# Attention ahead of two expert layers: two pairs of score banks that change roles from tile to tile, and chunks of the product with V that end with a tile

## The chip, the cores and the metric

The kernel runs on one core of a Trainium2 chip. The metric is the device time of one execution in microseconds (us); the kernel before has a median of 1350.61 us over three runs (1348.88 to 1350.84). A core has five engines that work side by side, each through its own queue in program order, and wait for each other by semaphores: TensorE (PE; its weight loads are listed apart as PEld), VectorE (DVE), ScalarE (ACT), GpSimd (POOL) and SyncE (SP, which here only starts transfers). Matmul results land in PSUM, which has eight banks; a bank holds 512 fp32 numbers in each of 128 partitions.

## The reference

The program computes attention and then two mixtures of experts. The change touches attention alone:

```
q_pool = q.reshape(B, H, S // 2, 2, D).mean(axis=3)      # B, H, S, D = 4, 8, 1152, 64
scores = scale * np.matmul(q_pool, k.transpose(0, 1, 3, 2))
scores = scores - np.max(scores, axis=-1, keepdims=True)
attn = np.exp(scores)
attn = attn / (np.sum(attn, axis=-1, keepdims=True) + 1e-09)
out = np.matmul(attn, v)
```

## The kernel before, in words

Two heads of one batch element make a pair; there are 16 pairs. A pair has 2 x 576 pooled queries, cut into nine tiles (t = 0 to 8) of 128, so there are 144 steps g = 9 * pair + t. A row of scores has 1152 entries, three parts of 384; each part fills most of a PSUM bank.

The list `SEQ` (line 17) says what each step issues, and in which order. Step g works on two tiles at once: it makes the scores, maxima and exponentials of tile g + 2, and takes tile g, whose exponentials lie in SBUF, through the rest.

- `qk(g+2, n)` (L158): matmuls of a score part. A part is the sum of two matmuls with 384 columns (for t = 4, whose rows belong to two heads, of four). `q0` makes the first two parts in the tile `Sa` (two banks, one buffer), `q1` the third in `Sb` (one bank, two buffers).
- `smax`, `bias` (L174, L177): DVE takes the maxima of `Sa` and of `Sb`, and of both the negative maximum `bs`.
- `exp` (L180): ACT takes the exponential of `Sa` (768 wide) and then of `Sb` (384 wide), each with a sum over the row; such an exponential is two instructions, ACTIVATE and ACTIVATION_READ_ACCUMULATOR, and the second one signals that the bank is free.
- `tp` (L212): PE transposes tile g in three groups of three into three `T` banks (L216). `evH` (L226): ACT rounds each group into `PH` (L227). `evL` (L228): DVE writes the remainder into `PL` (L229), which frees the `T` bank.
- `takeav` (L275): PE takes some of the pending matmuls with V (L239). The rows of a pair form four chunks of two or two and a half tiles; a chunk is 18 matmuls into the bank `O`, which has one buffer, and the last one is followed by a copy `O` to `xo` on ACT (L242). The table `AVN` says how many are taken at each t; they are taken in two halves, at `av` (between the second and the third cast on ACT) and at `aw` (behind the exponentials).
- `prep`, `inv`: transposes and copies for the pairs to come, which take a `T` bank too, and the transposed sums of the rows.

A step's `q0` may write `Sa` only when the step before has taken the exponential of its `Sa`. The eight banks are two for `Sa`, two for `Sb`, three for `T` and one for `O`. In the second half of the stage `dec` puts decoding of the expert weights into steps.

Of the kernel before, what the change touches and what calls it, by code (L numbers as in the profile page):

```python
# [10 lines left out]
F32=mybir.dt.float32; F32R=mybir.dt.float32r; I32=mybir.dt.int32; U32=mybir.dt.uint32; I64=mybir.dt.int64; BF16=mybir.dt.bfloat16  # L11
AF=mybir.ActivationFunctionType; ALU=mybir.AluOpType; AX=mybir.AxisListType
PSUM=bass.MemoryType.PSUM; DRAM=bass.MemoryType.DRAM

SEQ='q1 q0 m1 sum dec t0 c0 m0 pool scl t1 c1 bias l0 t2 av c2 l1 e0 e1 l2 aw prep inv st'.split()
AVN=(9,3,10,7,11,7,10,7,8)
PREP={0:((1,'T0'),),2:((1,'T1'),),3:((1,'T2'),),5:((1,'q2'),),7:((2,'q0'),),8:((2,'q1'),)}
POOL={0:((0,'vH1'),(0,'vL1')),1:((1,'H0'),(1,'L0')),3:((1,'H1'),(1,'L1')),4:((1,'H2'),(1,'L2')),5:((2,'qadd'),),6:((2,'qH'),(2,'qL')),8:((1,'vH0'),(1,'vL0'))}  # L20
SPQ={4:((1,'D0'),),7:((1,'D1'),)}
SCALE=(7,8,11,12)
CFG=dict(S2=1,S1=2,T=3,O=1)
def attention(tc, q, k, v, xS, rS, ident, pairs=None, extra=(), start=lambda: None):
    nc=tc.nc
    B,H,S,D=q.shape
    NP=H//2; SQ=S//2; KT=S//128
    if pairs is None: pairs=[(b,hp) for b in range(B) for hp in range(NP)]
    ctx=contextlib.ExitStack()
    with ctx:  # L30
# [4 lines left out]
        kv=ctx.enter_context(tc.tile_pool(name="a_kv",bufs=1))  # L35
        pr=ctx.enter_context(tc.tile_pool(name="a_pr",bufs=1))
        ld=ctx.enter_context(tc.tile_pool(name="a_ld",bufs=1))
        psS=ctx.enter_context(tc.tile_pool(name="a_psS",bufs=CFG['S2'],space=PSUM))
        psU=ctx.enter_context(tc.tile_pool(name="a_psU",bufs=CFG['S1'],space=PSUM))
        psT=ctx.enter_context(tc.tile_pool(name="a_psT",bufs=CFG["T"],space=PSUM))  # L40
        psO=ctx.enter_context(tc.tile_pool(name="a_psO",bufs=CFG["O"],space=PSUM))

# [6 lines left out]
        def load(i,what="qkv",eng=None):  # L49
            if i>=len(pairs): return  # L50
            b,hp=pairs[i]; h0=2*hp
            d=D_.setdefault(i,dict(ks={},vs={},kst={}))
            for w in what:
                if w=='q':
                    t=d['qn']=ld.tile([128,KT,2,D],F32,name="qn")
                    (eng or nc.sync).dma_start(out=t,in_=q[b,h0:h0+2].rearrange("h (s r) d -> (h s) (r d)",r=2).rearrange("(t p) x -> p t x",p=128))
                else:
                    t=d[w+'n']=ld.tile([128,2,KT,D],F32,name=w+"n")
                    (eng or nc.sync).dma_start(out=t,in_={'k':k,'v':v}[w][b,h0:h0+2].rearrange("h (p t) d -> p h t d",p=128))
# [89 lines left out]
        st={}  # L149
# [3 lines left out]
        def new(g):  # L153
            nm=sm.tile([128,2],F32,name="nm",bufs=3); bs=sm.tile([128,1],F32,name="bs",bufs=3)
            P=pp.tile([128,S],F32,name="P")
            st[g]=dict(nm=nm,bs=bs,su=sus[:,(g//9)%2,g%9],P=P,S={})

        def qk(g,n):  # L158
            i,t=divmod(g,9); d=D_[i]
            if g not in st: new(g)  # L160
            A=QA[i%2]; Bq=QB[i%2]
            if t==4: L=[(512,0),(640,1)]
            else: L=[(128*t,0)] if t<4 else [(128*t+128,1)]
            ops=[(w[:,c:c+128],h) for c,h in L for w in (A,Bq)]
            if n==0:
                o=psS.tile([128,2,512],F32,name="Sa"); st[g]['S'][0]=o[:,:,0:384]
                outs=[(o[:,j,0:384],j) for j in range(2)]
            else:
                o=psU.tile([128,384],F32,name="Sb"); st[g]['S'][1]=o
                outs=[(o,2)]  # L170
            for o,j in outs:
                for x,(w,h) in enumerate(ops):
                    nc.tensor.matmul(o,w,d['kst'][h][:,j*384:(j+1)*384],start=(x==0),stop=(x==len(ops)-1))  # L173
        def smax(g,n):  # L174
            s=st[g]
            nc.vector.tensor_reduce(out=s['nm'][:,n:n+1],in_=s['S'][n],axis=AX.XY if n==0 else AX.X,op=ALU.max,negate=True)  # L176
        def bias(g):  # L177
            nm=st[g]['nm']
            nc.vector.tensor_reduce(out=st[g]['bs'],in_=nm,axis=AX.X,op=ALU.min)  # L179
        def exp(g,n):  # L180
            s=st[g]; P=s['P']
            o=P[:,0:768].rearrange("p (c x) -> p c x",x=384) if n==0 else P[:,768:1152]
            nc.scalar.activation(out=o,in_=s['S'][n],func=AF.Exp,bias=s['bs'],scale=1.0,accum_out=s['su'][:,n:n+1])  # L183

        inv={}; rB={}
        TS=((0,5),(5,9))
# [4 lines left out]
        def invT(i,h):  # L191
            a,b=TS[h]; bb,hp=pairs[i]; n=b-a
            T=psT.tile([128,384],F32,name="T",tag="T")
            nc.tensor.transpose(T[0:n,0:128],inv.pop((i,h))[:,1,0:n],ident)
            o=sm.tile([5,128],F32,name="ro",bufs=1)
            nc.scalar.copy(out=o[0:n],in_=T[0:n,0:128])
            flat=rS[bb][hp:hp+1].rearrange("o h s -> (o h s)")
            nc.sync.dma_start(out=flat[128*a:128*b].rearrange("(t p) -> t p",p=128),in_=o[0:n])
        def invB(i,h):
            bb,hp=pairs[i]  # L200
            flat=rS[bb][hp:hp+1].rearrange("o h s -> (o h s)")
            r=rB[i,h]=sm.tile([128,576],F32,name="rB",bufs=2)
            nc.sync.dma_start(out=r,in_=flat[576*h:576*h+576].partition_broadcast(128))
# [8 lines left out]
        def tp(g,j):  # L212
            T=psT.tile([128,384],F32,name="T",tag="T"); P=st[g]['P']
            for n in range(3):
                kt=3*j+n
                nc.tensor.transpose(T[:,n*128:(n+1)*128],P[:,kt*128:(kt+1)*128],ident)  # L216
            st[g][j]=T
# [8 lines left out]
        def evH(g,j):  # L226
            for H,L,src in parts(g,j): nc.scalar.copy(out=H,in_=src)  # L227
# [29 lines left out]
        ops={}  # L257
        def do(i,*names):

            if i>=N: return  # L260
            if i not in ops: ops[i]=pool_ops(i,i==0)|prep_ops(i)
            for n in names:
                o=ops[i].pop(n,None)
                if o: o()
# [1 line left out]
        load(1)  # L266
        avq=[]; extra=list(extra); NX=len(extra); at={}
        for g in (0,1):
            for j in range(2): qk(g,j)
            if g==0: do(0,'k10','k11','k12','vH0','vL0','vH1','vL1'); do(1,'qadd','qH','qL')  # L270
            for j in range(2): smax(g,j)
            bias(g)
            for j in range(2): exp(g,j)
        DONE={1:[0],4:[1],6:[2],8:[3]}
        def takeav(n):  # L275
            while avq and n>0:
                avq[0].pop(0)(); n-=1
                if not avq[0]: avq.pop(0)
        stores=[]; sums={}
        for g in range(NG+4):  # L280
            i,t=divmod(g,9)
            if g<NG:
                if t==2 and i>0: load(i+1,'v')
                if t==2: load(i+2,'q')
                if t==5: load(i+2,'k')
            f2=g+2<NG; f0=g<NG
            if not f0:
                while avq: takeav(99)
            for op in SEQ:
                a=op[:-1]; n=op[-1]  # L290
                if op=='scl':
                    if g in at: x,y=at.pop(g); x(); stores.append((g,y))
                elif op=='st':
                    while stores and (stores[0][0]<g or not f0): stores.pop(0)[1]()
                elif op=='inv':
                    if f0 and t in (3,7): invT(i,t//4)
                    if t==5 and f0: invB(i,0)
                    if t==0 and i>0: invB(i-1,1)
                    for di,x in SPQ.get(t,()): f0 and do(i+di,x)
                    if g in (0,2): do(1,'q0' if g==0 else 'q1')  # L300
                elif not f0: pass
                elif a=='q': f2 and qk(g+2,int(n))
                elif a=='m': f2 and smax(g+2,int(n))
                elif a=='e': f2 and exp(g+2,int(n))
                elif op=='bias': f2 and bias(g+2)
                elif a=='t': tp(g,int(n))
                elif a=='c': evH(g,int(n))
                elif op in ('av','aw'): takeav((AVN[t]+(op=='av'))//2)
                elif a=='l': evL(g,int(n))
                elif op=='sum':  # L310
                    if t in (3,7): ssum(i,t//4)
                elif op in ('pool','prep'):
                    for di,n in (POOL if op=='pool' else PREP).get(t,()): do(i+di,n)
                elif op=='dec':
                    want=NX*max(0,g-70)//max(1,NG-74); take(extra,want-(NX-len(extra)))
                else: raise Exception(op)
            if f0:
                for c in DONE.get(t,[]): avq.append(av_ops(i,c))
# [702 lines left out]
```

## Time and profile before

| what | before |
|---|---|
| median of three runs | 1350.61 us |
| the profiled execution's own time | 1348.71 us |
| its span from the first to the last instruction | 1346.6 us |
| around the span | 2.1 us |
| PE busy / DVE busy / ACT busy | 1229.3 / 1095.5 / 892.2 us (91 / 81 / 66%) |
| granted TensorE clock, mean | 0.988 |

Attention takes about the first 570 us of the span. A busy share counts the time in which an instruction of the engine was under way. Matmuls overlap each other in it, and a weight load that waits for a semaphore may do so while the matmuls ahead of it still count as busy. So a stretch may show PE busy all the time and be set by something else; how long a step takes is read from the times at which the same instruction starts in one step and the next.

### The profile page before, as it was taken

The numbers are of one execution on the slowest core, as the hardware profiler recorded it, in microseconds if no ns is written. First come the engines' busy times: TensorE is split into PE (matmuls) and PEld (weight loads), VectorE is DVE, ScalarE is ACT, GpSimd is POOL, SyncE is SP. The second block draws the span as 40 slices with busy tenths as digits, with TensorE's granted clock in tenths as the row PEclk, the third lists the DMA queues.
The fourth block names the chain that finished last, engine by engine and source line by source line (L and its number), as shares of the span: only waits on it lengthen the run. The fifth ranks groups of instructions, "written<-read, shape, count | busy, mean of one in ns | idle before, by whom it ended". The sixth has DMA issues, their size and how long they took to land. (4 is left out here: it accounts for less than half of the span.)

```text
span 1346.6 us, 22379 instructions
## 1 busy us (share of the span) xinstructions
PE 1229.3 (91%) x7341; PEld 1084.1 (81%) x7341; DVE 1095.5 (81%) x1970; ACT 892.2 (66%) x2059; POOL 635.6 (47%) x567
## 2 busy tenths in 40 slices
PE   5999999999999999977768989899999999999997
PEld 4888888888888888865657879797989887788885
DVE  5788888888888888789997697848485889998894
ACT  6888888888888888744445645454556657576772
POOL 3444444444555555256667443424342435455852
PEclk9999999999999999989898999999999999999999
DMA  5554555556555575244331311010101323258710
GB/s 165 141 143 127 128 154 138 139 142 168 152 151 137 132 187 140 58 139 117 109 102 48 109 41 36 25 40 16 40 17 47 138 72 138 94 191 328 278 36 22
DMA packets 119624, 154.34 MB, mean 115 GB/s; under 512 B 12135, under 2 KB 93943, under 8 KB 115152
## 3 DMA queue, kind: packets, MB, share of 16 engines
q1 hardware_dynamic: 115232, 140.93, 36.7%
q0 software_dynamic: 3696, 11.34, 2.4%
q8 instruction: 60, 0.98, 0.3%
q10 hardware_dynamic: 576, 0.59, 0.1%
q14 instruction: 60, 0.49, 0.1%
HBM read 155.48 MB, written 20.28 MB: 131 GB/s over the span
## 5 line engine op out<-in xcount | busy, mean ns | idle before, releaser
L430 PE MATMUL h<-xH,W 128*128 128x384 f32 (+1 forms) x896 | 229.0, 327 | 51.5 <-ACT yt L439 37.5
L227 ACT CAST PH<-T 128x384 fp32r<-128x384 f32 (+1 forms) x480 | 185.7, 460 | 84.7 <-PE T L216 84.6
L229 DVE TENSOR_TENSOR PL<-T,PH 128x384 fp32r<-128x384 f32 (+1 forms) x480 | 217.4, 508 | 6.4 <-ACT PH L227 6.3
L430 PEld LDWEIGHTS h<-xH,W 128*128 128x128 f32 x896 | 161.8, 195 | 72.3 <-ACT yt L439 48.3
L453 POOL TENSOR_TENSOR gL<-et,gH 128x384 fp32r<-128x384 f32 (+1 forms) x112 | 120.1, 1072 | 197.7 <-ACT gH L452 170.1
L818 DVE TENSOR_TENSOR W<-sg,W 128x2048 fp32r<-128x2048 f32 (+1 forms) x84 | 193.9, 2341 | 14.1 <-POOL W L816 7.2
L435 ACT ACTIVATE em<-h 128x384 f32<-128x384 f32 (+1 forms) x112 | 49.8, 445 | 224.4 <-DVE et L444 149.5
L239 PE MATMUL O<-PH,vs 128*128 128x256 f32 (+1 forms) x576 | 166.3, 311 | 17.9 <-ACT xo L242 17.9
L176 DVE TENSOR_REDUCE nm<-Sa 128x1 f32<-128x768 f32 x144 | 136.8, 950 | 40.6 <-PE Sa L173 35.1
L216 PE MATMUL T<-ident,P 128*128 128x128 f32 x1296 | 164.8, 272 | 0.0
L239 PE MATMUL O<-PL,vs 128*128 128x256 f32 (+1 forms) x576 | 161.9, 303 | 0.0
L216 PEld LDWEIGHTS T<-ident,P 128*128 128x128 f32 x1296 | 150.1, 140 | 5.2
L430 PE MATMUL h<-xL,W 128*128 128x384 f32 (+1 forms) x448 | 144.0, 321 | 0.7 <-DVE xL L385 0.7
L444 DVE SCALAR_TENSOR_TENSOR et<-em,et 128x384 f32<-128x384 f32 (+1 forms) x112 | 69.5, 621 | 84.4 <-ACT em L441 82.8
L183 ACT ACTIVATE P<-Sa,bs 128x768 f32<-128x768 f32 x144 | 133.6, 928 | 4.1 <-DVE bs L179 3.9
L173 PE MATMUL Sa<-kst,qa 128*128 128x384 f32 x320 | 114.5, 358 | 16.7 <-ACT P L183 14.8
L239 PEld LDWEIGHTS O<-PH,vs 128*128 128x128 f32 x576 | 108.6, 189 | 25.6 <-ACT xo L242 23.9
L817 ACT CAST W<-sg 128x2048 fp32r<-128x2048 f32 (+1 forms) x63 | 114.2, 1835 | 15.0 <-DMA sg<-moe_w 15.0
L461 PE MATMUL y<-W,gH 128*128 128x512 f32 x288 | 115.7, 402 | 0.0
L176 DVE TENSOR_REDUCE nm<-Sb 128x1 f32<-128x384 f32 x144 | 79.8, 554 | 42.6 <-PE Sb L173 41.7
L462 PE MATMUL y<-W,gH 128*128 128x512 f32 x288 | 113.8, 395 | 0.0
L239 PEld LDWEIGHTS O<-PL,vs 128*128 128x128 f32 x576 | 108.8, 189 | 0.0
(298 smaller groups left out, 2940.9 us busy)
## 6 DMA issues: line engine op xcount, KB each, us to landing
sg<-moe_w SPq DMA_DIRECT2D x80, 1024.0 KB
qn<-q SPq DMA_DIRECT2D x16, 576.0 KB
kn<-k SPq DMA_DIRECT2D x16, 576.0 KB
rB<-rS SPq DMA_DIRECT2D x32, 288.0 KB
vn<-v SPq DMA_DIRECT2D x15, 576.0 KB
dx<-moe_w_in SPq DMA_DIRECT2D x16, 512.0 KB
dx<-moe_w_out SPq DMA_DIRECT2D x16, 512.0 KB
qb<-qa SPq DMA_DIRECT2D x64, 96.0 KB
```

Of the source, the lines that this page charges most:

```text
L173: nc.tensor.matmul(o,w,d['kst'][h][:,j*384:(j+1)*384],start=(x==0),stop=(x==len(ops)-1))
L176: nc.vector.tensor_reduce(out=s['nm'][:,n:n+1],in_=s['S'][n],axis=AX.XY if n==0 else AX.X,op=ALU.max,negate=True)
L183: nc.scalar.activation(out=o,in_=s['S'][n],func=AF.Exp,bias=s['bs'],scale=1.0,accum_out=s['su'][:,n:n+1])
L216: nc.tensor.transpose(T[:,n*128:(n+1)*128],P[:,kt*128:(kt+1)*128],ident)
L227: for H,L,src in parts(g,j): nc.scalar.copy(out=H,in_=src)
L229: for H,L,src in reversed(list(parts(g,j))): nc.vector.tensor_tensor(out=L,in0=src,in1=H.bitcast(F32),op=ALU.subtract)
L239: nc.tensor.matmul(O[0][:,:n],vs[:,kt].rearrange("p a d -> p (a d)"),R[:,kt,:n],start=first,stop=last)
L430: nc.tensor.matmul(h[:,:N],a,b[:,k,:N],start=(n==0),stop=(n==11)); n+=1
L453: nc.gpsimd.tensor_tensor(out=gL[:,:N],in0=t_,in1=gH[:,:N].bitcast(F32),op=ALU.subtract)
L461: nc.tensor.matmul(y,gH[:,sl],wH,start=(f==0),stop=False)
L817: else: nc.scalar.copy(out=H[:,q],in_=s[:,q])
L818: (nc.gpsimd if (w,j,h) in self.pool_L else nc.vector).tensor_tensor(out=L[:,q],in0=s[:,q],in1=H[:,q].bitcast(F32),op=ALU.subtract)
```

## The change

It has three parts.

1. The tiles `Sa` and `Sb` are replaced by two pairs of banks, `S0` and `S1`. Tile g has its first two parts in the pair `S(g mod 2)` and its third in the first bank of the other pair. The parts are computed in the order 0, 1, 2 (`q0 q1 q2` in `SEQ`); the maximum of the first two is taken before that of the third; and the exponential of the third part (384 wide, "short") now stands ahead of that of the first two (768 wide, "long").
2. `AVN` is rewritten so that each chunk's last matmul is the last one that a step takes.
3. The transposes for the middle third of a pair's queries (`q1` in `PREP`) move from t = 8 to t = 0, where `T0` already stands.

```diff
-SEQ='q1 q0 m1 sum dec t0 c0 m0 pool scl t1 c1 bias l0 t2 av c2 l1 e0 e1 l2 aw prep inv st'.split()
-AVN=(9,3,10,7,11,7,10,7,8)
+SEQ='q0 q1 q2 m1 sum dec t0 c0 m0 pool scl t1 c1 bias l0 t2 av c2 l1 e0 e1 l2 aw prep inv st'.split()
+AVN=(6,3,9,7,11,8,10,8,10)
...
-        psS=ctx.enter_context(tc.tile_pool(name="a_psS",bufs=CFG['S2'],space=PSUM))
-        psU=ctx.enter_context(tc.tile_pool(name="a_psU",bufs=CFG['S1'],space=PSUM))
+        psS=ctx.enter_context(tc.tile_pool(name="a_psS",bufs=1,space=PSUM))
...
+        SB=[psS.tile([128,2,512],F32,name=f"S{n}") for n in range(2)]
...
-            for o,j in outs:
-                for x,(w,h) in enumerate(ops):
-                    nc.tensor.matmul(o,w,d['kst'][h][:,j*384:(j+1)*384],start=(x==0),stop=(x==len(ops)-1))
+            o=SB[g%2][:,n,0:384] if n<2 else SB[1-g%2][:,0,0:384]
+            for x,(w,h) in enumerate(ops):
+                nc.tensor.matmul(o,w,d['kst'][h][:,n*384:(n+1)*384],start=(x==0),stop=(x==len(ops)-1))
+        def score(g,n): return SB[1-g%2][:,0,0:384] if n==0 else SB[g%2][:,:,0:384]
...
-            o=P[:,0:768].rearrange("p (c x) -> p c x",x=384) if n==0 else P[:,768:1152]
-            nc.scalar.activation(out=o,in_=s['S'][n],func=AF.Exp,bias=s['bs'],scale=1.0,accum_out=s['su'][:,n:n+1])
+            o=P[:,768:1152] if n==0 else P[:,0:768].rearrange("p (c x) -> p c x",x=384)
+            nc.scalar.activation(out=o,in_=score(g,n),func=AF.Exp,bias=s['bs'],scale=1.0,accum_out=s['su'][:,n:n+1])
```

PE in the step t = 7 of the first pair, before; `O_1070` is the chunk that is under way and `O_1177` the next one.

```order
L173 MATMUL Sb_1142<-kst_1032,qa0_135 128x384
L173 MATMUL Sb_1142<-kst_1032,qb0_137 128x384
L173 MATMUL Sa_1145<-kst_1032,qa0_135 128x384
L173 MATMUL Sa_1145<-kst_1032,qb0_137 128x384
L173 MATMUL Sa_1145<-kst_1032,qa0_135 128x384
L173 MATMUL Sa_1145<-kst_1032,qb0_137 128x384
L216 MATMUL T_1154<-ident_75,P_1042 128x128 x3
L216 MATMUL T_1163<-ident_75,P_1042 128x128 x3
L216 MATMUL T_1170<-ident_75,P_1042 128x128 x3
L239 MATMUL O_1070<-PL_879,vs_715 128x320
L239 MATMUL O_1177<-PH_992,vs_772 128x320
```

The same step now; `S0` and `S1` are the two pairs, and `O_1138` is the next chunk.

```order
L168 MATMUL S0_141<-kst_999,qa0_132 128x384
L168 MATMUL S0_141<-kst_999,qb0_134 128x384
L168 MATMUL S0_141<-kst_999,qa0_132 128x384
L168 MATMUL S0_141<-kst_999,qb0_134 128x384
L168 MATMUL S1_142<-kst_999,qa0_132 128x384
L168 MATMUL S1_142<-kst_999,qb0_134 128x384
L211 MATMUL T_1118<-ident_75,P_1009 128x128 x3
L211 MATMUL T_1127<-ident_75,P_1009 128x128 x3
L211 MATMUL T_1134<-ident_75,P_1009 128x128 x3
L234 MATMUL O_1138<-PH_959,vs_745 128x320
```

The four matmuls of the pair come first and the two of the third part last; the chunk before has ended in the step before, so the step's first product opens a new one. The first `S0` matmul waits for the short exponential of the step before, and the first `S1` matmul for the long one, which has read that pair.

ACT in a step of the first pair in which a chunk ends, before.

```order
L227 CAST PH_768<-T_764 128x3x128
L227 CAST PH_768<-T_775 128x3x128
L242 COPY xo_790<-O_668 128x320
L227 CAST PH_768<-T_782 128x3x128
L183 ACTIVATE P_754,sus_141<-Sa_758,bs_753 128x768
L183 ACTIVATE P_754,sus_141<-Sb_755,bs_753 128x384
```

ACT in a step of the first pair in which a chunk ends, now.

```order
L222 CAST PH_850<-T_846 128x3x128
L222 CAST PH_850<-T_855 128x3x128
L222 CAST PH_850<-T_862 128x3x128
L178 ACTIVATE P_832,sus_138<-S0_141,bs_831 128x384
L178 ACTIVATE P_832,sus_138<-S1_142,bs_831 128x768
L237 COPY xo_880<-O_759 128x256
```

The copy of `O` has moved from between the casts to behind the exponentials, and the short exponential from behind the long one to before it.

## Rows read from the trace of the kernel before

**Rows 1.** Waits of PE, 30 to 570 us: total us, times, longest.
```profile
PE O L239 <- ACT xo L242: 17.3, 31, 0.7
PE Sa L173 <- ACT P L183: 10.3, 19, 1.6
```

**Rows 2.** Nine steps of one pair, by windows: length, busy us by engine, clock, DMA.
```profile
213.42:216.93 3.51, 3.51 (x26) 3.30 (x25) 3.06 (x6) 2.98 (x8) 0.76 (x2) 1.00 0.99 243
216.93:220.45 3.52, 3.52 (x27) 3.42 (x26) 3.02 (x7) 2.79 (x8) 1.34 (x1) 1.00 0.65 171
220.45:224.77 4.32, 3.76 (x27) 3.47 (x26) 3.19 (x9) 3.59 (x10) 2.56 (x3) 1.00 0.11 30
224.77:228.32 3.55, 3.55 (x28) 3.47 (x27) 3.07 (x7) 3.02 (x9) 3.13 (x4) 1.00 0.47 96
228.32:232.68 4.36, 3.80 (x28) 3.46 (x27) 3.15 (x7) 3.53 (x10) 0.00 (x0) 1.00 0.94 210
232.68:236.88 4.20, 3.69 (x25) 3.34 (x24) 3.03 (x7) 2.77 (x8) 2.40 (x3) 1.00 0.83 248
236.88:240.44 3.56, 3.56 (x30) 3.49 (x29) 3.02 (x7) 3.03 (x9) 0.00 (x0) 1.00 0.53 153
240.44:243.96 3.52, 3.52 (x28) 3.15 (x26) 3.20 (x9) 3.31 (x10) 2.23 (x3) 1.00 0.00 0
243.96:247.66 3.70, 3.57 (x28) 3.21 (x27) 3.23 (x10) 3.30 (x13) 2.90 (x3) 1.00 0.50 113
```

**Rows 3.** Timeline of PE, 215 to 220 us: start, length, engine, line, operation.
```profile
215.68 0.42 PE L173 MATMUL Sb<-kst,qa 128*128 128x384 f32 x1
...
216.13 0.44 PE L173 MATMUL Sa<-kst,qa 128*128 128x384 f32 x1
...
219.38 0.34 PE L173 MATMUL Sb<-kst,qa 128*128 128x384 f32 x1
...
219.74 0.35 PE L173 MATMUL Sa<-kst,qa 128*128 128x384 f32 x1
```

**Rows 4.** Timeline of ACT, 213 to 217 us.
```profile
213.95 1.25 ACT L227 CAST PH<-T 128x384 fp32r<-128x384 f32 x3 [0.56 <-PE T L216]
215.06 0.93 ACT L183 ACTIVATE P<-Sa,bs 128x768 f32<-128x768 f32 x1
215.86 0.22 ACT L183 ACTIVATION_READ_ACCUMULATOR P<-Sa,bs 128x1 f32 x1
215.95 0.60 ACT L183 ACTIVATE P<-Sb,bs 128x384 f32<-128x384 f32 x1
216.41 0.23 ACT L183 ACTIVATION_READ_ACCUMULATOR P<-Sb,bs 128x1 f32 x1
```

**Rows 5.** Timeline of PE, 222 to 236 us.
```profile
222.29 0.41 PE L239 MATMUL O<-PH,vs 128*128 128x320 f32 x1 [0.56 <-ACT xo L242]
...
235.39 0.44 PE L173 MATMUL Sa<-kst,qa 128*128 128x384 f32 x1 [0.51 <-ACT P L183]
```

**Rows 6.** Timeline of ACT, 230 to 246 us.
```profile
230.12 0.42 ACT L242 COPY xo<-O 128x320 f32<-128x320 f32 x1 [0.42 <-issue]
...
230.82 0.92 ACT L183 ACTIVATE P<-Sa,bs 128x768 f32<-128x768 f32 x1
...
234.32 0.93 ACT L183 ACTIVATE P<-Sa,bs 128x768 f32<-128x768 f32 x1
...
245.75 0.97 ACT L183 ACTIVATE P<-Sa,bs 128x768 f32<-128x768 f32 x1
```

**Rows 7.** Timeline of DVE, 217 to 220 us.
```profile
217.13 0.96 DVE L176 TENSOR_REDUCE nm<-Sa 128x1 f32<-128x768 f32 x1 [0.25 <-PE Sa L173]
218.12 0.16 DVE L179 TENSOR_REDUCE bs<-nm 128x1 f32<-128x2 f32 x1
218.19 1.48 DVE L229 TENSOR_TENSOR PL<-T,PH 128x384 fp32r<-128x384 f32 x3
219.94 0.56 DVE L176 TENSOR_REDUCE nm<-Sb 128x1 f32<-128x384 f32 x1 [0.27 <-PE Sb L173]
```

More of the change, by code (lines that the diff above doesn't have):

```diff
@@ L13 @@
 PSUM=bass.MemoryType.PSUM; DRAM=bass.MemoryType.DRAM
-SEQ='q1 q0 m1 sum dec t0 c0 m0 pool scl t1 c1 bias l0 t2 av c2 l1 e0 e1 l2 aw prep inv st'.split()
-AVN=(9,3,10,7,11,7,10,7,8)
-PREP={0:((1,'T0'),),2:((1,'T1'),),3:((1,'T2'),),5:((1,'q2'),),7:((2,'q0'),),8:((2,'q1'),)}
+SEQ='q0 q1 q2 m1 sum dec t0 c0 m0 pool scl t1 c1 bias l0 t2 av c2 l1 e0 e1 l2 aw prep inv st'.split()
+AVN=(6,3,9,7,11,8,10,8,10)
+PREP={0:((1,'q1'),(1,'T0')),2:((1,'T1'),),3:((1,'T2'),),5:((1,'q2'),),7:((2,'q0'),)}
 POOL={0:((0,'vH1'),(0,'vL1')),1:((1,'H0'),(1,'L0')),3:((1,'H1'),(1,'L1')),4:((1,'H2'),(1,'L2')),5:((2,'qadd'),),6:((2,'qH'),(2,'qL')),8:((1,'vH0'),(1,'vL0'))}
@@ L22 @@
 SCALE=(7,8,11,12)
-CFG=dict(S2=1,S1=2,T=3,O=1)
+CFG=dict(T=3,O=1)
 def attention(tc, q, k, v, xS, rS, ident, pairs=None, extra=(), start=lambda: None):
@@ L164, in qk @@
             ops=[(w[:,c:c+128],h) for c,h in L for w in (A,Bq)]
[L165 to L170, printed above, removed]
-            for o,j in outs:
-                for x,(w,h) in enumerate(ops):
-                    nc.tensor.matmul(o,w,d['kst'][h][:,j*384:(j+1)*384],start=(x==0),stop=(x==len(ops)-1))
+            o=SB[g%2][:,n,0:384] if n<2 else SB[1-g%2][:,0,0:384]
+            for x,(w,h) in enumerate(ops):
+                nc.tensor.matmul(o,w,d['kst'][h][:,n*384:(n+1)*384],start=(x==0),stop=(x==len(ops)-1))
+        def score(g,n): return SB[1-g%2][:,0,0:384] if n==0 else SB[g%2][:,:,0:384]
         def smax(g,n):
-            s=st[g]
-            nc.vector.tensor_reduce(out=s['nm'][:,n:n+1],in_=s['S'][n],axis=AX.XY if n==0 else AX.X,op=ALU.max,negate=True)
+            nc.vector.tensor_reduce(out=st[g]['nm'][:,n:n+1],in_=score(g,n),axis=AX.X if n==0 else AX.XY,op=ALU.max,negate=True)
         def bias(g):
@@ L268, in attention @@
         for g in (0,1):
-            for j in range(2): qk(g,j)
+            for j in range(3): qk(g,j)
             if g==0: do(0,'k10','k11','k12','vH0','vL0','vH1','vL1'); do(1,'qadd','qH','qL')
-            for j in range(2): smax(g,j)
+            for j in (1,0): smax(g,j)
             bias(g)
@@ L299, in attention @@
                     for di,x in SPQ.get(t,()): f0 and do(i+di,x)
-                    if g in (0,2): do(1,'q0' if g==0 else 'q1')
+                    if g==0: do(1,'q0')
                 elif not f0: pass
```

## The prediction

> **What bounds the kernel now.** I read the waits first. Within attention PE names two: 17.3 us before the first product with V of a new chunk, until ACT has copied the bank `O`, and 10.3 us before the scores, until ACT has taken an exponential [rows 1]. That looks like an engine near its limit with 28 us to win. The windows say something else. I cut one pair at the start of each step's first transpose (L216), call that moment T, and get the nine steps from t = 5 round to t = 4, in all 34.24 us [rows 2]. The reader should see that four of them last 3.51, 3.52, 3.52 and 3.56 us although their work on PE differs, and that in them PE counts as busy from end to end. Equal lengths with unequal work mean that a loop through several engines sets the step, and the timelines give its parts:
>
> - From T = 213.42 the casts begin at 213.95 and follow each other; the exponential of `Sa` begins at 215.06, which is T + 1.64 [rows 2, 4]. I call this moment E.
> - Its accumulator read ends at 215.86 + 0.22 = 216.08, E + 1.02 [rows 4]. Only then is `Sa` free.
> - The first matmul into `Sa` starts at 216.13, 0.05 later, though `Sb` was begun at 215.68 [rows 3].
> - The next T is 216.93, so four score matmuls that start from a wait take 0.80 [rows 2, 3]. Where nothing waited, from 219.74 to 220.45, they took 0.71 [rows 2, 3].
>
> The sum, 1.64 + 1.02 + 0.05 + 0.80 = 3.51, is the step. The same sum fits the odd steps. For t = 1 the next scores are those of the tile over two heads: 235.39 to 236.88 is 1.49 for eight matmuls [rows 2, 5], so each further one costs (1.49 - 0.80)/4 = 0.17, and 1.64 + 1.02 + 0.05 + 1.49 = 4.20, as measured. For t = 4 there are six casts, E is at 245.75 - 243.96 = 1.79 [rows 2, 6], and the sum is 3.66 against 3.70. For t = 0 the copy to `xo` at 230.12 stands between the casts [rows 6], E comes at 230.82 - 228.32 = 2.50, and the sum is 4.37 against 4.36. Only t = 7 (4.32) is longer than this loop: there the new chunk waits 0.56 at 222.29 [rows 5] on PE itself. So attention is bound by the loop PE, ACT, PE through the score banks, and not by PE's work.
>
> **What the change removes.** Chunks that end with a step take the copy to `xo` out from between the casts, and no product waits for it: the copy now has the rest of the step. The steps t = 0 and t = 7 then fall to the length of an ordinary step. The same 72 products per pair are issued, and PE has room for them: the step with most of them has ten of 320 columns and no other transposes, now as before, and PE came to its end at 219.38, T + 2.45 [rows 2, 3].
>
> **What it adds.** Exponential order and bank roles lengthen the loop. Both exponentials are done when the second accumulator read ends, 216.41 + 0.23 = 216.64, E + 1.58 [rows 4]; the order of the two doesn't change that sum. Before, the second one freed a bank with a spare, and nobody waited. Now the second one is the long one, and it frees the bank into which the very next step's third part goes. The first one is short: from its start to the end of its read it takes 216.41 + 0.23 - 215.95 = 0.69 [rows 4], so it frees the bank for `q0` at E + 0.69.
>
> So the next step goes: `q0` can start at E + 0.74 (that is T + 2.38), or when PE comes free, at most T + 2.45. Four matmuls end 0.80 or 0.71 later, in either case by about E + 1.54. `q2` must wait until E + 1.58 + 0.05 = E + 1.63, and its two matmuls, which again start from a wait, take 0.80 - 2 x 0.17 = 0.46. An ordinary step becomes 1.64 + 1.63 + 0.46 = 3.73 instead of 3.51. Put the other way: the freeing moment comes 0.56 later, and only two matmuls instead of four (0.34) are left behind it.
>
> For t = 1 the first wait decides, since eight matmuls stand before the third part: 1.64 + 0.74 + 1.49 + 4 x 0.17 = 4.56. For t = 4 I add the same 0.22 to the measured 3.70, which gives 3.92.
>
> **What lies beside other work.** DVE's part stays hidden. Before, the long maximum starts at T + 0.20 and the bias ends at 218.12 + 0.16, T + 1.35, so 0.29 before E [rows 2, 7]. Now the long maximum needs only the first four matmuls. These end two matmuls and a short wait before T, so it starts about T - 0.25; with 0.96 for it, 0.56 and 0.03 for the short one and 0.16 for the bias [rows 7] it ends at about T + 1.46, still 0.18 before E. The lower bound of its cost is nothing (E is set by the casts, so an earlier bias gains nothing either). The upper bound is the long maximum starting at T + 0.20 all the same: T + 1.91, so 0.27 in each step. I take nothing, being nearer to the four-matmul start that the instruction order gives it.
>
> In t = 0 two groups of three transposes now follow the products; each takes a `T` bank and so waits for a subtraction on DVE. In the sample step those begin at T + 1.26 and three take 1.48 [rows 2, 7], so the second bank comes free at about T + 2.3, and even with 0.4 for the last group the scores start by T + 2.7 and `q2` by T + 3.4, against T + 3.27 from the loop: the step ends at T + 3.75 instead of 3.73 (two unwaited matmuls take 0.35). I cost it at nothing; if the second group had to wait for all three subtractions, it would be some 0.4 us per pair, 6 us in all. Nothing is gained there, as the loop is longer than PE's work. The transfers that follow the moved transposes fill query buffers a whole pair ahead of their use and wait for nobody. On ACT the two copies and the one of `T0` follow the exponentials, where ACT otherwise waits (0.56 us at 213.95, [rows 4]).
>
> **The sum.** Seven ordinary steps at 3.73, plus 4.56 and 3.92, are 34.59 us a pair against 34.24, so 0.35 more: t = 0 and t = 7 give back 0.63 and 0.59, and the seven others take 0.17 to 0.36 each. Over 16 pairs that is 5.6. Corrections at the ends: the first pair has no chunk to end at t = 0, so it saves nothing there (0.63 + 0.21 = 0.8 more); the last pair's t = 8 has no scores left to compute (0.2 less); and four products and one copy's wait go from the tail of the stage (4 x 0.15 + 0.56 = 1.2 less). Net 5.0. The profiled execution took 1348.71 us, so the sum is 1353.7 us for it. The median shown is 1.9 above that execution; the same change from 1350.61 gives 1355.6 us, which I forecast. Its own range, 0.03 us a step either way over 142 steps, is 1351 to 1360.
>
> **Rivals.**
>
> - *PE is the bound after all.* Then the wait for `xo` is gained whole and the loop stays hidden: 1350.6 - 17.3 = 1333.3 us. For it speaks that PE counts as busy all through ordinary steps; against it that these steps are equal to 0.05 us and equal to the loop's sum. Chance 0.08. The Trainium skill's page "Perfetto Trace Analysis", section "Identifying the Most-Contended Engine", says to take the engine with the highest occupancy as the bottleneck, with a caution about TensorE, and to close the gaps on it; by that rule this rival would be the forecast, and the trace does not bear it out here.
> - *The second wait costs no restart.* If the weights for `q2` are loaded during the short wait, its two matmuls take 0.09 less (0.80 against 0.71). In eight steps of a pair that is 0.72, over 16 pairs 11.5: 1344 us, faster than before. Against it: each first matmul that followed a wait for the bank was long (0.44 against 0.35, [rows 3, 5]). Chance 0.12.
> - *The maxima arrive late*, as bounded above: 0.27 x 9 x 16 = 39, so 1394 us. It decides once the long maximum waits for the third part. Chance 0.04.
> - *The two transpose groups in t = 0 hold PE*: 1362 us. Chance 0.04.
> - *The more frequent waits lower the clock.* Against it: the granted clock is 1.00 (its upper level, 2.4 GHz) in all nine windows, with waits of 0.56 and 0.51 us in them [rows 2, 5]. At the lower level, 1.2 GHz, PE's 2.45 + 6 x 0.17 = 3.5 us of an ordinary step would double, an estimate of 3.3 us more a step and of some 470 us in all, if it lasted: 1820 us. Chance 0.01. The Trainium skill's page "TensorE: Matmul & The Clock Gate", section "A second HAM failure mode: psum-queue depth-cycling", describes a kernel whose PE paused briefly between groups of matmuls as it went through its banks, and kept losing clock; the trace of before shows none of that here.
>
> The change does what it says: the instruction order shows every copy to `xo` behind the exponentials. The remaining 0.03 is for gains and losses that cancel.
>
> **How the numbers follow.** The forecast has 0.68. A measurement of this kernel can tell about 0.2%, 2.7 us, from no change, so slower begins at 1353.3. Of the forecast's 0.68 I put 0.08 below that line; the other 0.60 and the three slower rivals' 0.09 make 0.69. Within 0.2%: 0.08 + 0.03 = 0.11. Faster: 0.08 + 0.12 = 0.20. The range goes from 1343, which takes in the rival without a restart, to 1361; outside stay PE as the bound, the late maxima and the held transposes, 0.17 with the clock.
>
> **What would show it.** In the profile after, no wait of a product for `xo`; the windows from T to T of t = 0 and t = 7 near 3.73, of t = 1 near 4.56, of t = 2, 3, 5, 6 and 8 near 3.73; the first matmul of the third part starting 0.05 after the long exponential's accumulator read, with a length of about 0.44; and the exponentials beginning at T + 1.64 everywhere. Ordinary steps of 3.6 or less, or E later than T + 1.7, would make the forecast wrong.

## The result and the profile after

The changed kernel takes 1364.87 us, median of four runs (1363.26 to 1366.16), beside 1350.38 us for the kernel before, measured next to it (four runs). The ratio is 1.0109, with a 95% interval of 1.0091 to 1.0126: slower, by 14.5 us, where 5.0 were forecast. The span of the profiled execution went from 1346.6 to 1362.0 us. The direction and the mechanism in the steady steps came out as predicted; the cost of the decoding was left out of the sum, and so was the clock at the start.

The nine steps of one pair after the change, t = 5 round to t = 4, cut from T to T as in [rows 2] (length, busy us of PE, PEld, DVE, ACT and POOL with counts, granted clock, DMA share, GB/s):

```profile
218.73:222.46 3.73, 3.73 (x27) 3.46 (x26) 2.95 (x7) 3.08 (x8) 0.83 (x2) 1.00 0.96 267
222.46:226.21 3.75, 3.75 (x27) 3.42 (x26) 3.00 (x7) 3.02 (x8) 1.26 (x1) 1.00 0.45 125
226.21:229.94 3.73, 3.73 (x29) 3.45 (x28) 3.05 (x9) 3.17 (x9) 2.51 (x3) 1.00 0.05 19
229.94:233.67 3.73, 3.73 (x27) 3.41 (x26) 3.09 (x7) 3.02 (x8) 3.20 (x4) 1.00 0.45 91
233.67:237.41 3.74, 3.74 (x29) 3.31 (x28) 2.83 (x7) 3.22 (x10) 0.00 (x0) 1.00 0.71 155
237.41:241.99 4.58, 3.69 (x25) 3.45 (x24) 3.27 (x7) 2.99 (x8) 1.52 (x2) 1.00 0.60 139
241.99:245.72 3.73, 3.73 (x28) 3.34 (x27) 2.82 (x7) 3.20 (x9) 0.88 (x1) 1.00 0.97 298
245.72:249.45 3.73, 3.63 (x27) 3.16 (x26) 3.05 (x9) 3.32 (x10) 2.27 (x4) 1.00 0.18 45
249.45:253.37 3.92, 3.75 (x27) 3.29 (x26) 3.34 (x10) 3.14 (x11) 2.87 (x3) 1.00 0.57 122
```

All seven ordinary steps last 3.73 to 3.75 us, t = 1 4.58 and t = 4 3.92. The pair takes 34.64, where 34.59 was predicted. PE again counts as busy from end to end in nearly every step, and nearly every step is 0.2 us longer: it still is not the bound.

The first of these steps on ACT and PE, T = 218.73 (start, length, engine, line, operation), answers to [rows 3, 4]:

```profile
219.26 1.24 ACT L222 CAST PH<-T 128x384 fp32r<-128x384 f32 x3 [0.77 <-PE T L211]
220.38 0.61 ACT L178 ACTIVATE P<-S,bs 128x384 f32<-128x384 f32 x1
220.85 0.22 ACT L178 ACTIVATION_READ_ACCUMULATOR P<-S,bs 128x1 f32 x1
220.94 0.92 ACT L178 ACTIVATE P<-S,bs 128x768 f32<-128x768 f32 x1
221.73 0.23 ACT L178 ACTIVATION_READ_ACCUMULATOR P<-S,bs 128x1 f32 x1
```

```profile
221.14 0.43 PE L168 MATMUL S<-kst,qa 128*128 128x384 f32 x1
...
222.01 0.44 PE L168 MATMUL S<-kst,qa 128*128 128x384 f32 x1
222.29 0.34 PE L168 MATMUL S<-kst,qb 128*128 128x384 f32 x1
222.46 1.15 PE L211 MATMUL T<-ident,P 128*128 128x128 f32 x9
```

E is at T + 1.65. The long read ends at 221.73 + 0.23 = 221.96, E + 1.58; the third part starts 0.05 later with a long first matmul (0.44), and 0.45 after that the next T follows: 1.65 + 1.58 + 0.05 + 0.45 = 3.73. Each length is within 0.01 of the predicted one. DVE in the same step, as in [rows 7]:

```profile
218.38 1.42 DVE L171 TENSOR_REDUCE nm<-S 128x1 f32<-128x768 f32 x2 [0.55 <-PE S L168]
219.84 0.16 DVE L174 TENSOR_REDUCE bs<-nm 128x1 f32<-128x2 f32 x1
```

Both maxima run without a break from T - 0.35 on, and the bias ends at 220.00, T + 1.27, which leaves 0.38 us up to E.

The waits of PE in attention, 30 to 590 us (total us, times, longest), answer to [rows 1]:

```profile
PE S L168 <- ACT P L178: 23.2, 29, 1.7
...
PE O L234 <- ACT xo L237: 0.6, 1, 0.6
```

The wait for `xo` is gone, 17.3 us to 0.6. That gain was real; the longer loop swallows it.

Where the 15.4 us of span went, by the times of T in both traces: up to T of the third tile 2.4 (30.82 to 33.21 us); from there the pairs that decoding leaves alone, up to T of t = 5 in the last pair, 5.3 (353.41 to 358.72 in all); pairs 8 to 12, where decoding lengthens steps, 8.4 (174.53 to 182.90); from T of t = 5 in the last pair to the end -0.7.

Of the 8.4, the steady pair's 0.39 (34.64 against 34.25) explains five times that, 2.0. The rest, 6.4 us, is new. Put the other way: these five pairs exceed five steady ones by 3.3 us before and by 9.7 now. One such step shows why. It is t = 4 of pair 11, T = 429.10; the next T is at 434.01, so it lasts 4.91 instead of 3.92. First DVE, then ACT:

```profile
428.89 0.96 DVE L171 TENSOR_REDUCE nm<-S 128x1 f32<-128x768 f32 x1 [0.60 <-PE S L168]
429.77 1.43 DVE L345 SCALAR_TENSOR_TENSOR dx<-dx 128x512 f32<-128x512 int32 x1
431.12 0.54 DVE L171 TENSOR_REDUCE nm<-S 128x1 f32<-128x384 f32 x1
431.70 0.15 DVE L174 TENSOR_REDUCE bs<-nm 128x1 f32<-128x2 f32 x1
```

```profile
429.84 1.22 ACT L222 CAST PH<-T 128x192 fp32r<-128x192 f32 x5
431.95 0.58 ACT L178 ACTIVATE P<-S,bs 128x384 f32<-128x384 f32 x1 [0.89 <-DVE bs L174]
```

`SEQ` has `dec` between `m1` and `m0`. A decoding instruction of 1.43 us stands between the long and the short maximum, the bias ends at 431.85, and the exponentials start at T + 2.85 with 0.89 us of waiting on ACT. This one takes more than the 0.38 us that an ordinary step has to spare. Before, [rows 7] shows DVE idle for 0.27 and 0.25 ahead of each maximum, and the short one came first: there was room for most of it.

The start of attention, windows as above. After the change:

```profile
20.00:22.00 2.00, 0.59 (x2) 0.59 (x3) 0.61 (x2) 1.32 (x3) 1.83 (x3) 0.70 0.54 200
22.00:24.00 2.00, 2.00 (x9) 1.91 (x8) 0.91 (x2) 0.24 (x2) 0.62 (x1) 0.50 0.00 0
24.00:26.00 2.00, 2.00 (x10) 1.66 (x9) 1.70 (x5) 1.30 (x3) 0.00 (x0) 0.50 0.00 0
26.00:28.00 2.00, 2.00 (x12) 1.85 (x11) 0.64 (x2) 2.00 (x8) 0.00 (x0) 0.59 0.00 0
```

The same stretch before:

```profile
20.00:22.00 2.00, 0.01 (x1) 0.01 (x1) 1.28 (x4) 1.05 (x3) 1.83 (x3) 1.00 0.51 192
22.00:24.00 2.00, 1.93 (x13) 1.66 (x13) 0.98 (x2) 1.18 (x4) 0.52 (x1) 1.00 0.00 0
```

The granted clock fell to 0.50, which is 1.2 GHz, from 20.80 to 27.63 us; in this trace of the kernel before, it stayed at 1.00.

### The profile page after: what moved, and what is told of

The parts are those of the page before. It is cut to its first block, busy times and chain, and to the rows that moved or that the text cites. A ratio compares the mean times of both kernels' runs of the same rounds, so it can differ in the third digit from the quotient of the medians.

```text
span 1362.0 us, 22402 instructions
## 1 busy us (share of the span) xinstructions
PE 1247.3 (92%) x7341; PEld 1084.2 (80%) x7341; DVE 1087.7 (80%) x1970; ACT 891.1 (65%) x2059; POOL 633.5 (47%) x567
## 5 line engine op out<-in xcount | busy, mean ns | idle before, releaser
L171 DVE TENSOR_REDUCE nm<-S 128x1 f32<-128x768 f32 (+1 forms) x288 | 208.0, 750 | 109.8 <-PE S L168 109.8
L222 ACT CAST PH<-T 128x384 fp32r<-128x384 f32 (+1 forms) x480 | 182.8, 460 | 102.8 <-PE T L211 102.3
L178 ACT ACTIVATE P<-S,bs 128x384 f32<-128x384 f32 (+1 forms) x288 | 214.6, 764 | 8.8 <-DVE bs L174 8.6
L168 PE MATMUL S<-kst,qa 128*128 128x384 f32 x480 | 185.7, 387 | 27.6 <-ACT P L178 26.4
L813 DVE TENSOR_TENSOR W<-sg,W 128x2048 fp32r<-128x2048 f32 (+1 forms) x84 | 190.3, 2298 | 17.6 <-ACT W L812 9.7
L168 PE MATMUL S<-kst,qb 128*128 128x384 f32 x480 | 162.8, 339 | 0.0
L234 PE MATMUL O<-PL,vs 128*128 128x256 f32 (+1 forms) x576 | 158.7, 299 | 0.0
L168 PEld LDWEIGHTS S<-kst,qa 128*128 128x128 f32 x480 | 90.8, 189 | 62.6 <-ACT P L178 56.4
```

Source lines behind the costliest of these rows:

```text
L168: nc.tensor.matmul(o,w,d['kst'][h][:,n*384:(n+1)*384],start=(x==0),stop=(x==len(ops)-1))
L171: nc.vector.tensor_reduce(out=st[g]['nm'][:,n:n+1],in_=score(g,n),axis=AX.X if n==0 else AX.XY,op=ALU.max,negate=True)
L178: nc.scalar.activation(out=o,in_=score(g,n),func=AF.Exp,bias=s['bs'],scale=1.0,accum_out=s['su'][:,n:n+1])
L234: nc.tensor.matmul(O[0][:,:n],vs[:,kt].rearrange("p a d -> p (a d)"),R[:,kt,:n],start=first,stop=last)
L813: (nc.gpsimd if (w,j,h) in self.pool_L else nc.vector).tensor_tensor(out=L[:,q],in0=s[:,q],in1=H[:,q].bitcast(F32),op=ALU.subtract)
```

## The experiments

Ratios are against the kernel before, measured next to each kernel, with 95% intervals.

**Decoding taken out from between the maxima** (the changed kernel):

```diff
-... m1 sum dec t0 c0 m0 ... e0 e1 l2 aw ...
+... m1 sum t0 c0 m0 ... e0 e1 l2 dec aw ...
```

> The changed kernel with one edit: the decoding of the expert weights (dec) stands behind the last subtraction of a step instead of between the long and the short maximum. Theory (decode between the maxima makes the bias and with it the exponentials late): in the pairs 8 to 12 the steps fall back to 3.73, 4.57 and 3.92 us but for a few, the 9.7 us that these pairs lie above 5 x 34.64 shrink to under 3, and the kernel takes about 1358 us. Rival (the decoding costs the same wherever it stands, through VectorE's time or a shared port): 1365 us, within 1.5. In the first 30 us the stretch at half clock stays, as nothing changes there.

Measured: 1356.32 us (1354.93 to 1356.52, five runs), 1.0042 [1.0028, 1.0056]. Pairs 8 to 12 now exceed five steady pairs by 1.9 us instead of 9.7, and ACT's waits for the bias from 300 to 480 us drop from the first row (after) to the second (this kernel):

```profile
ACT P L178 <- DVE bs L174: 6.8, 15, 0.9
```

```profile
ACT P L178 <- DVE bs L174: 0.9, 2, 0.6
```

The steady pair (34.60) stays as it was, and the start still has a stretch at clock 0.50 (first T at 24.00); here it begins at 17.45 us, ahead of the second tile's scores. So the place of `dec` costs the changed kernel 8.5 us; how much of that the change itself brought, the next run tells.

**The same edit on the kernel before.**

> The kernel before with one edit: the decoding stands behind the last subtraction of a step. Theory (before, the short maximum came first and VectorE then waited for the scores of the long one, so that part of a decoding instruction fell into that wait): the pairs 8 to 12 lie only 3.3 us above 5 x 34.25 in the kernel before, so at most that can be won: about 1347.5 us. Rival (decoding between the maxima cost as much before as it does in the changed kernel): 8.5 us less, about 1342.

Measured: 1347.99 us (nine runs), 0.9976 [0.9966, 0.9986]. Next to it the kernel before took 1350.99 us, so before the change `dec` cost 3.0 us at the same place. The difference of the two runs, 8.5 - 3.0 = 5.5, is what the change made of it, near the 6.4 of the accounting. With `dec` out of the way in both, the change costs 1356.32 - 1347.99 = 8.3 us: the loop and the start.

**The tables alone, on the kernel before:** new `AVN` and `PREP`, old banks and orders.

```diff
-AVN=(9,3,10,7,11,7,10,7,8)
-PREP={0:((1,'T0'),),...,7:((2,'q0'),),8:((2,'q1'),)}
+AVN=(6,3,9,7,11,8,10,8,10)
+PREP={0:((1,'q1'),(1,'T0')),...,7:((2,'q0'),)}
...
-                    if g in (0,2): do(1,'q0' if g==0 else 'q1')
+                    if g==0: do(1,'q0')
```

> The kernel before with only the tables of the change (AVN, and q1 of PREP moved to t = 0): score banks, their order and the exponentials as before. Theory (loop through the banks; the tables save, the banks cost): the steps t = 0 and t = 7 fall to 3.52 us, the others stay as before, a pair takes 32.6 us instead of 34.24, and the kernel about 1325 us. Rival (the tables cost, by two groups of transposes in t = 0 or by the products' places): 1350 us or more.

Measured: 1331.24 us (1330.92 to 1333.3, four runs), 0.9863 [0.9846, 0.988]. This half of the change is worth 19 us, and the other half costs 34. Three steps of a pair, t = 7, 8 and 0:

```profile
215.27:218.91 3.64, 3.64 (x28) 3.57 (x27) 3.17 (x9) 3.13 (x10) 2.01 (x3) 1.00 0.11 25
218.91:222.43 3.52, 3.52 (x27) 3.40 (x25) 3.10 (x7) 3.05 (x9) 3.44 (x4) 1.00 0.39 82
222.43:226.19 3.76, 3.73 (x28) 3.35 (x27) 3.03 (x7) 3.26 (x11) 0.25 (x1) 1.00 0.79 168
```

In [rows 2] t = 7 and t = 0 took 4.32 and 4.36. They fall, but not to 3.52: with the shorter loop of the old banks, t = 0's two groups of transposes hold PE after all (3.76), the rival that the changed kernel's loop of 3.73 had hidden. Why t = 7 takes 3.64 was not taken apart. A pair takes 32.93 instead of the 32.6 expected.

**The banks and orders alone:** the changed kernel with the old tables.

> The changed kernel with the tables of before (AVN, PREP): only the score banks, their order and the order of maxima and exponentials are changed. Theory: ordinary steps 3.73, t = 0 at 2.50 + 1.63 + 0.46 = 4.59, t = 7 about 4.33, t = 1 4.56, t = 4 3.92, a pair 36.05 us against 34.24, so 28 us, with some 8 us for the decoding and the start: about 1387 us. Rival (the banks cost little, the tables most): near 1350 us.

Measured: 1384.21 us (1381.97 to 1384.78, four runs), 1.0247 [1.0229, 1.0266]. Steps t = 6 to t = 1:

```profile
228.92:232.65 3.73, 3.73 (x26) 3.41 (x25) 2.98 (x7) 2.69 (x7) 1.10 (x1) 1.00 0.59 137
232.65:237.00 4.35, 3.79 (x27) 3.49 (x26) 3.01 (x9) 3.59 (x10) 2.99 (x4) 1.00 0.05 16
237.00:240.74 3.74, 3.74 (x28) 3.46 (x27) 3.16 (x7) 3.14 (x9) 2.70 (x3) 1.00 0.49 101
240.74:245.31 4.57, 4.01 (x28) 3.48 (x27) 3.04 (x7) 3.49 (x9) 0.05 (x1) 1.00 0.89 211
245.31:249.89 4.58, 3.69 (x25) 3.45 (x24) 3.13 (x7) 2.69 (x7) 2.36 (x3) 1.00 0.86 263
```

An ordinary step is 3.73 here too: the added 0.2 belongs to banks and orders and not to the tables. The steady pair measured 36.06, as expected. The price of decoding belongs to this half as well: pairs 8 to 12 exceed five steady ones by 9.0 us here, and by 4.1 with the tables alone.

**The long exponential first again,** in the changed banks (`e1 e0` for `e0 e1`).

> The changed kernel with the two exponentials of a step exchanged: long first, short second. Nothing else. Theory (the step is set by the moment at which the bank for the next matmuls comes free): the bank for q0 is now free only at E + 1.63 and all six matmuls stand behind that, so an ordinary step is 1.64 + 1.63 + 0.80 + 0.35 = 4.42 us, t = 1 5.45, t = 4 4.6, and the kernel takes about 1463 us. Rival (the work of the engines, not the order of release, sets the step): 1365 us.

Measured: 1478.76 us, one run. Ordinary steps last 4.43; the profile's step of T = 217.79 on ACT and on PE:

```profile
219.43 0.93 ACT L178 ACTIVATE P<-S,bs 128x768 f32<-128x768 f32 x1
...
220.78 0.23 ACT L178 ACTIVATION_READ_ACCUMULATOR P<-S,bs 128x1 f32 x1
```

```profile
221.06 0.45 PE L168 MATMUL S<-kst,qa 128*128 128x384 f32 x1 [0.63 <-ACT P L178]
```

All six score matmuls now wait for the second read, 221.01, and the first starts 0.05 later. Given these banks, the short exponential first is right: it saves 0.7 us a step. The total went 16 us past the expected 1463: t = 3 and t = 7 last 4.58 since sums delay the bias, and the clock falls in some steps of the steady stretch too (0.85 in the mean of one of 6.30 us). How much each of the two is worth was not taken apart.

**The start.** In the changed kernel PE has six score matmuls at 18.0 to 19.5 us and then waits 1.88 us; before, it had two more (the spare `Sb` let it begin the third part of the next tile) and waited 2.08. The theory: those matmuls kept the clock. Two kernels put unread ones into a `T` bank, in the changed kernel, once; they leave nothing out. In the first, four ahead of the second tile's scores and four behind them:

> The changed kernel with eight more matmuls that nobody reads, four before and four behind the scores of the second tile, where TensorE otherwise waits. Theory (the first steps of the changed kernel are longer because TensorE, with six instead of eight score matmuls before its long wait, drops to half clock there): the granted clock is 1.00 from 20 to 28 us, the third tile's first transpose comes at about 31 us after the span's start instead of 33.2, and the kernel takes 2.2 us less, about 1362.6. Rival (the first steps are longer because of the banks' waits and the three groups of transposes in the first step): 33 us and 1365.

Measured: 1362.99 us (1362.0 to 1365.56, five runs), 1.0088 [1.0074, 1.0102]. The clock was 0.50 from 15.26 to 18.67 us, beginning ahead of the added matmuls (17.23), and 1.00 after that; T of the third tile came at 32.22 instead of 33.21. Half the gain: the four in front, begun at half clock, delayed the scores from 18.03 to 18.72. So the second has only the four behind:

```diff
+            if g==1:
+                T=psT.tile([128,384],F32,name="T",tag="T")
+                for x in range(4): nc.tensor.matmul(T,QA[0][:,0:128],D_[0]['kst'][0][:,0:384],start=True,stop=True)
```

> The changed kernel with four more matmuls that nobody reads, behind the scores of the second tile alone, so that they delay nothing. Theory (the first steps lose to the half clock): granted clock 1.00 up to 28 us, the first transpose of the first tile at about 22.6 us after the span's start instead of 23.5, that of the third tile at about 31.3 instead of 33.2, and the kernel near 1363. Rival (the clock falls before, in the wait ahead of the second tile's scores, whatever comes behind): 23.5 and 33.

Measured: 1363.14 us (1362.86 to 1363.55, four runs), 1.0098 [1.0081, 1.0115]. First the changed kernel's PE at the start, then this one's:

```profile
21.41 0.69 PE L168 MATMUL S<-kst,qa 128*128 128x384 f32 x1 [1.88 <-ACT P L178]
21.89 0.53 PE L168 MATMUL S<-kst,qb 128*128 128x384 f32 x1
```

```profile
19.28 0.86 PE L267 MATMUL T<-kst,qa 128*128 128x384 f32 x4
21.33 0.44 PE L168 MATMUL S<-kst,qa 128*128 128x384 f32 x1 [1.19 <-ACT P L178]
21.61 0.34 PE L168 MATMUL S<-kst,qb 128*128 128x384 f32 x1
```

The clock stays at 1.00, the matmul is 0.34 instead of 0.53, and T of the third tile comes at 31.41 instead of 33.21, 1.8 us earlier. That much is shown in the trace; the totals (1.7 us less than the changed kernel's, intervals overlapping) agree with it and would not prove it. The remaining 0.6 us is the longer loop: with the clock at 1.00, t = 0 and t = 1 of the first pair last 4.16 and 4.58 us, against 3.82 and 4.21 before, and the first T comes 0.1 earlier.

That the two missing score matmuls made the clock fall is not shown, and the other traces speak against it as the whole cause. Three kernels described below have the old banks, all eight score matmuls and a wait of 2.09 us behind them, and their clock fell as well: to 0.50 at 22.87 us (`dec` behind the exponentials), 23.30 (the long exponential ahead of the third cast) and 22.90 (`T0` moved). The first of them, windows as above:

```profile
22.00:24.00 2.00, 1.90 (x10) 1.84 (x11) 0.82 (x1) 0.80 (x4) 0.64 (x1) 0.72 0.00 0
24.00:26.00 2.00, 2.00 (x10) 1.58 (x10) 1.80 (x5) 1.68 (x4) 0.00 (x0) 0.50 0.00 0
```

In all, the clock fell in the first 30 us in three of the six traces with the old banks, and in all four with the new banks and nothing added, at 15.86 to 20.80 us; two of these four, and the trace with eight matmuls added, fell ahead of the second tile's scores, as the rival of the last run has it. With one trace of each kernel, what four added matmuls do to it stays open.

**Towards a better kernel.** Three variants of the tables-alone kernel. With `dec` behind the exponentials as well:

> The kernel before with the tables of the change and the decoding behind the last subtraction: banks and exponentials as before. Theory: 1331.2 less most of the 4.8 us by which its pairs 8 to 13 lie above the others, about 1327 us. Rival: no gain over 1331.

Measured: 1331.52 us (1330.03 to 1335.69, four runs), 0.9862 [0.9844, 0.988]: no gain over 1331.24 that can be measured. In the traces pairs 8 to 13 gain 2.2 us, and the start, with the clock at 0.50, takes 0.7 of it back (T of the third tile at 31.92 instead of 31.24).

With the long exponential ahead of the third cast besides (`e0 c2 l1 e1 l2` for `c2 l1 e0 e1 l2`), so that `Sa` is free sooner:

> d_avndec with the long exponential ahead of the third cast and the short one behind it. Theory (the loop through the banks sets the step, and the casts set when the exponential can start): the exponential starts when the bias is there, at about T + 1.41 instead of T + 1.64, ordinary steps fall from 3.52 to what TensorE's own work allows (3.3 to 3.55), t = 1 to 3.97, a pair to 31.3 to 32, and the kernel to 1305 to 1318 us. Rival (another limit stands close behind, TensorE or the transposes' banks, which come free later): 1325 to 1330.

Measured: 1349.85 us (1347.72 to 1350.88, eleven runs), 0.9987 [0.9978, 0.9996]. The expectation failed, its rival too. Waits of DVE and of ACT, 30 to 560 us:

```profile
DVE PL L229 <- ACT PH L227: 80.6, 140, 0.9
```

```profile
ACT P L183 <- DVE bs L179: 42.8, 83, 1.4
```

The later cast makes DVE's third subtraction wait in nearly every step (140 times, 0.58 us each); the maxima queued behind it come late, and with them the bias on which that very exponential waits. The loop had only been moved to DVE. A steady pair takes 33.56 us against 32.92, some 10 us in all, and pairs 8 to 12 exceed five of them by 10.9 us, against 2.0 in the kernel that this one was made from.

With `dec` and the exponentials as in the tables-alone kernel, and `T0`'s transposes moved from t = 0 to t = 1:

```diff
-PREP={0:((1,'q1'),(1,'T0')),2:((1,'T1'),),...
+PREP={0:((1,'q1'),),1:((1,'T0'),),2:((1,'T1'),),...
-POOL={...,1:((1,'H0'),(1,'L0')),...
+POOL={...,2:((1,'H0'),(1,'L0')),...
```

> b_avn (the kernel before with the tables of the change) with T0 moved from t = 0 to t = 1, where only three products stand, and the rounding of its result on GpSimd a step later. Theory (with the short loop of before, the two groups of transposes in t = 0 hold TensorE for 0.24 us, which the longer loop of the changed kernel hid): t = 0 falls from 3.76 to 3.52 us, t = 1 stays at 4.21, and the kernel takes about 3.7 us less than b_avn, 1327.5. Rival (the wait moves to t = 1): no gain over 1331.

Measured: 1329.35 us (1328.58 to 1332.05, four runs), 0.9854 [0.9838, 0.9871]. Its steps t = 0 and t = 1:

```profile
220.99:224.51 3.52, 3.50 (x25) 3.00 (x24) 3.10 (x7) 3.02 (x10) 0.36 (x1) 1.00 0.84 180
224.51:228.85 4.34, 3.97 (x29) 3.73 (x27) 3.06 (x6) 3.22 (x9) 0.57 (x2) 1.00 0.60 142
```

t = 0 falls from 3.76 to 3.52 as expected; t = 1 takes half of it back (4.22 to 4.34). Its interval overlaps that of the tables alone. Both beat the kernel before and the changed one: keep the old banks and take the new tables.

## Why the prediction was right or wrong

- **The loop through the score banks: right.** Seven steps of 3.73, one of 4.56 and one of 3.92 were predicted; 3.73 to 3.75, 4.58 and 3.92 came. The run with the old tables shows the same added 0.2, and the one with the long exponential first the sum for that order (4.43). Without decoding, the pairs lost 5.3 us, and the first pair's t = 0 and t = 1, counted in the start above, 0.6 more, where the sum had 11 x 0.35 + 0.8 - 0.2 = 4.5. Of the excess 0.7 is one step (t = 1 of pair 4, 5.24 us): ACT's copy to `KX` waited 0.86 us for a transfer, up to 168.28 us.
- **The removed wait: right.** t = 0 and t = 7 went to 3.74 and 3.73. The tables are worth 1350.57 - 1331.24 = 19 us with the old banks and 1384.21 - 1364.87 = 19 with the new.
- **"DVE's part stays hidden": this step failed.** It holds in steps without decoding, where the bias even ends earlier than worked out (T + 1.27, not 1.46). I counted only the maxima and left out `dec`, which stands between them in the `SEQ` that I had quoted. Before, the maximum ahead of `dec` was the short one, available early; now it is the long one, with 0.38 us to spare. The term at nothing measured 6.4 us, and the two runs that move `dec` confirm it (5.5 by their totals).
- **The clock: the rival was priced for the steady steps only,** where it never came (1.00 in all nine windows). It came for 6.83 us at the start, which the sum had left out, and cost 1.8 of the 2.4 us there: with four matmuls added and the clock at 1.00, T of the third tile came at 31.41 instead of 33.21. Why it fell stays open. It fell at the start of three kernels with the old banks as well, so it is not shown that these 1.8 us come of the change rather than of the one execution that was profiled. The Trainium skill's page "TensorE: Matmul & The Clock Gate", section "A second HAM failure mode: psum-queue depth-cycling", tells of a kernel that lost clock over and over in brief pauses between groups of matmuls; the steady steps of this trace, each of which waits for a bank at 1.00, do not show it.
- **The tail: mis-sized,** -0.9 instead of -1.2 (the -0.7 above has the 0.2 of one ordinary step in it).
- **PE as the bound, a second wait without a restart, late maxima in every step:** none of them came (3.73, first matmul 0.44, bias at T + 1.27).

Predicted 4.5 + 5 x 0.35 - 1.2 = 5.0; measured 5.3 + 8.4 + 2.4 - 0.7 = 15.4. Of the missing 10.4, decoding is 6.4 and the clock at the start 1.8, together 8.2; the rest is the step of pair 4, the tail, and differences of a few tenths that were not taken apart.

## What to carry to other kernels

Where steps with unequal work have equal lengths, find the loop through the engines and add it up from one step's timeline; such a sum held here to 0.02 us in the steady steps that the loop sets. Then ask what else passes through the queues on that loop in other stretches of the program, since a slack of 0.38 us that is ample in one pair is gone in the next. And a change of two parts is worth undoing by halves: here one half gains 19 us and the other loses 34.

## What was not expected of the hardware

- The clock at the start: after six score matmuls and within a wait of 1.88 us it fell to 0.50. After eight and a wait of 2.08 or 2.09 us it stayed at 1.00 in three traces and fell to 0.50 in three others. In the steady steps 0.89 us without work on PE (t = 1: 4.58 less 3.69) left it at 1.00. Neither the length of the wait nor the matmuls ahead of it decide alone. With the long exponential first, a wait of 1.78 us was followed by matmuls of 0.34, and only 1.1 us later by matmuls of 0.52.
- A bank is released at the end of ACTIVATION_READ_ACCUMULATOR, not of ACTIVATE: where PE waited for the bank, the next matmul started 0.05 us after it, before and after the change.
- The same decoding instruction (L345) took 1.43 us between the maxima and 0.68 where it stood behind the subtractions (427.13 us in the run with `dec` moved). Beside the first, POOL ran two TENSOR_TENSORs on SBUF (429.64 to 432.47 us); beside the second it was idle. The Trainium skill's page "SBUF — State Buffer", section "SBUF: two separate sides", says that DVE with two SBUF inputs and GpSimd exclude each other on a shared port; these two rows agree with it. So do the others: of the 152 decoding instructions of this kind between 300 and 560 us in the twelve traces, 40 took over 0.72 us, and each of the 40 ended 0.53 to 0.55 us after the end of the POOL instruction that was under way at its start; the other 112 took 0.65 to 0.69. No run was made to test it.
